# A fused linear-attention and mixer kernel: a subtraction on VectorE, tiles sorted by size, early reciprocals by way of DRAM, and products without a reader behind the early groups

## The chip, the cores and the metric

The kernel runs on one core of one Trainium2 chip. A core has a matrix engine (TensorE, in the profile PE, with PEld for its weight loads), and VectorE (DVE), ScalarE (ACT), GpSimd (POOL) and SyncE (SP), each with its own in-order queue of instructions. All data loads of the steady part are issued from SP. On chip, data lies in SBUF or in the eight banks of PSUM, into which the products are written. The metric is the device time of one execution in microseconds (us): the median of 3 runs of the kernel before is 1182.55 us.

## The reference, cut to what matters

```python
# q, k, v: (8, 8, 576, 64) float32; w_phi: (64, 128)
def phi(x):
    proj = np.einsum('bhsd,df->bhsf', x, w_phi)
    proj = proj - np.max(np.abs(proj), axis=-1, keepdims=True)
    return np.concatenate([np.exp(proj), np.exp(-proj)], axis=-1)
q_p, k_p = phi(q), phi(k)
kv = np.einsum('bhsf,bhsd->bhfd', k_p, v)
z = np.sum(k_p, axis=2)
num = np.einsum('bhsf,bhfd->bhsd', q_p, kv)
den = np.einsum('bhsf,bhf->bhs', q_p, z)[..., None] + 1e-06
x = (num / den)                      # then (B, S, H * D) = (8, 576, 512)
h = np.maximum(x.T @ w_tok1, 0.0) @ w_tok2        # token mixing, 576 -> 256 -> 576
u = x + h.T
out = u + np.maximum(u @ w_ch1, 0.0) @ w_ch2      # channel mixing, 512 -> 1536 -> 512
```

The subtraction in `phi` (the largest magnitude of a row off each of its 128 values) and the reciprocal of `den` are what the change touches.

## The kernel before, in words

There are 32 head pairs, numbered i = 0 to 31: four pairs (`NP`) for each of the eight batch entries. Five streams of work are written as Python generators and woven together by `weave` (L556): the keys of each pair (`keys`, L262: projection, subtraction, two exponentials `kp`, then products with v that sum up in `pkv`), its queries (`queries`, L325: projection, subtraction, transpose `pt`, exponentials `qf`, then the numerator products `pn` in `numerators`, L384), the token mixing of a batch entry, the loading of the mixer's weights (`load_weights`, L144), and the channel mixing. A planner then sets the order of the instructions on every engine when the program is built, from its own estimates of durations; on the chip each engine takes its queue in that order.

The weights come as float64. `convert` (L114) loads a block into one of four staging buffers, takes the magnitude on ACT (L131), rebuilds float32 bits on DVE in four instructions (L132 to L135), writes the rounded high part on ACT and the low part on POOL (`split`, L69 to L75). The 24 blocks of the channel weights are named `wc`.

The first four pairs (i < `PLAIN`) are computed with plain float32 products; `EARLY` = 8 covers the pairs of the first two batch entries. A group of keys or queries of an early plain pair goes through `less_max` (L191): one or two projections into half of a PSUM bank (L216), the row maximum on DVE (L226, `mx`), its negation on POOL (L229, `nmx`), and then, for keys, four ACT exponentials straight from PSUM that add `nmx` or `mx` as a bias, one for each unit and sign (L285); for queries an ACT pass for each unit that adds `nmx` (L235) and writes `pm`. From pair 4 on the values are subtracted on POOL (L237). Each plain pair has five groups of keys and five of queries: four with two units and one with one unit.

`numerators` takes one half of the sequence (k = 0: 320 columns, k = 1: 256) in two steps j. The rows of a `pn` bank hold 64 numerator rows and 64 copies of one denominator row; ACT copies the numerators into `x` (L404), the denominators plus 1e-6 go to `den` (L406 on ACT for the early pairs, L408 on DVE later). After j = 1 the reciprocal of the full 128-partition `den` is taken on DVE (L410) and POOL multiplies (L411). Token mixing begins with transposes of `x` (L432).

SBUF tiles come from two pools. Tiles that the matrix engine streams (`streamed`, L55) are padded by 16 elements on either side, and small columns to 32 elements (`column`, L65), so that every address keeps its offset within 128 bytes.

## Time and profile before

| | |
|---|---|
| median of 3 runs | 1182.55 us (1182.36 to 1184.48) |
| the profiled execution's own time | 1180.86 us |
| its span, first to last instruction | 1178.9 us |
| PE busy | 1134.0 us, 96% |
| DVE busy | 702.9 us, 60% |
| ACT busy | 673.5 us, 57% |
| POOL busy | 584.8 us, 50% |
| mean granted TensorE clock | 0.976 |

The spans leave out 2.0 us of the execution around the first and the last instruction. "Busy" counts an instruction from its start to its end, waits for a shared port included; a matrix product's end is modelled, so that products overlap. In the tables of groups, `out<-in` names the tiles, the count stands behind an x, then come total busy time, the mean in ns of one, and the idle time of the engine before them with what ended it. In the tables by stretch of time each engine's busy time has its count of instructions in brackets; then come the granted clock, the busy share of the DMA engines and their GB/s.

### The profile page before, as it was taken

The numbers are of one execution on the slowest core, as the hardware profiler recorded it, in microseconds if no ns is written. First come the engines' busy times: TensorE is split into PE (matmuls) and PEld (weight loads), VectorE is DVE, ScalarE is ACT, GpSimd is POOL, SyncE is SP. The second block draws the span as 40 slices with busy tenths as digits, with TensorE's granted clock in tenths as the row PEclk, the third lists the DMA queues.
The fourth block names the chain that finished last, engine by engine and source line by source line (L and its number), as shares of the span: only waits on it lengthen the run. The fifth ranks groups of instructions, "written<-read, shape, count | busy, mean of one in ns | idle before, by whom it ended". The sixth has DMA issues, their size and how long they took to land.

```text
span 1178.9 us, 24080 instructions
## 1 busy us (share of the span) xinstructions
PE 1134.0 (96%) x9032; PEld 1099.9 (93%) x9032; DVE 702.9 (60%) x1406; ACT 673.5 (57%) x1913; POOL 584.8 (50%) x774
## 2 busy tenths in 40 slices
PE   8877999999999999999999999999999999999998
PEld 6655889998999999998999999999999989999998
DVE  6899783566746666657656565474665666553111
ACT  6988784575746565566646455563665666441110
POOL 3567783465636564565546355462554655430000
PEclk9877799999999999999999999999999999999999
DMA  9543120111101111111111011110111110000000
GB/s 232 177 142 113 31 78 2 49 32 49 31 19 38 42 31 40 41 40 41 31 48 33 19 32 49 31 50 7 43 32 49 40 40 11 19 1 19 19 19 18
DMA packets 65299, 54.30 MB, mean 46 GB/s; under 512 B 44768, under 2 KB 56416, under 8 KB 65184
## 3 DMA queue, kind: packets, MB, share of 16 engines
q1 hardware_dynamic: 63824, 52.41, 15.4%
q8 instruction: 71, 1.16, 0.4%
q10 hardware_dynamic: 1360, 0.36, 0.1%
q14 instruction: 44, 0.36, 0.1%
HBM read 43.32 MB, written 9.44 MB: 45 GB/s over the span
## 4 chain that ended last, share of the span: by engine, by line
PE 84%; DVE 6%; ACT 6%; issue 2%; POOL 1%; DMA 1%; SPq 0%; POOLq 0%; DVEq 0%; ACTq 0%
PE acc L81 26%; PE h L81 26%; PE pkv L308 8%; PE pn L81 7%; PE ph L81 4%; PE pa L81 3%; PE pt L364 2%; PE ppk L212 2%; PE ppq L212 2%; DVE bitsc L135 1%; DVE bitsc L134 1%; PE px L432 1%; DVE bitsc L132 1%; ACT kp L285 1%; DVE den L410 1%
## 5 line engine op out<-in xcount | busy, mean ns | idle before, releaser
L81 PE MATMUL acc<-gh,wc 128*128 128x256 f32 x1728 | 339.7, 283 | 0.1
L81 PEld LDWEIGHTS acc<-gh,wc 128*128 128x128 f32 x1728 | 274.4, 188 | 0.4 <-ACT gh L498 0.4
L81 PE MATMUL h<-ul,wc_h 128*128 128x256 f32 x864 | 245.4, 284 | 1.9 <-POOL ul L479 1.8
L81 PE MATMUL h<-uh,wc_h 128*128 128x256 f32 x864 | 245.7, 285 | 0.5 <-DVE gl L499 0.5
L81 PE MATMUL h<-uh,wc_l 128*128 128x256 f32 x864 | 244.2, 283 | 0.0
L81 PE MATMUL acc<-gl,wc 128*128 128x256 f32 x864 | 243.2, 284 | 0.0
L308 PE MATMUL pkv<-v,kp 128*128 128x65 f32 (+1 forms) x1152 | 166.7, 280 | 6.9 <-ACT kp L285 4.3
L378 POOL TENSOR_TENSOR ql<-qf,qh 128x320 fp32r<-128x320 f32 (+1 forms) x112 | 93.0, 830 | 160.2 <-ACT qh L377 160.0
L308 PEld LDWEIGHTS pkv<-v,kp 128*128 128x128 f32 x1152 | 157.1, 202 | 14.6 <-ACT kp L285 7.9
L81 PEld LDWEIGHTS h<-ul,wc_h 128*128 128x128 f32 x864 | 162.8, 188 | 3.1 <-POOL ul L479 3.1
L81 PEld LDWEIGHTS h<-uh,wc_h 128*128 128x128 f32 x864 | 162.4, 188 | 1.1 <-DVE gl L499 1.1
L81 PEld LDWEIGHTS h<-uh,wc_l 128*128 128x128 f32 x864 | 163.2, 189 | 0.0
L81 PEld LDWEIGHTS acc<-gl,wc 128*128 128x128 f32 x864 | 162.9, 188 | 0.0
L499 DVE SCALAR_TENSOR_TENSOR gl<-h,gh 128x512 fp32r<-128x512 f32 x108 | 74.0, 685 | 144.1 <-ACT gh L498 143.1
L371 ACT ACTIVATE qf<-pt 128x320 f32<-128x320 f32 (+1 forms) x256 | 105.5, 416 | 85.9 <-PE pt L364 84.6
L282 ACT ACTIVATE kp<-pmk 128x256 f32<-128x256 f32 x280 | 96.0, 392 | 72.7 <-POOL pmk L237 69.6
L498 ACT ACTIVATE gh<-h 128x512 fp32r<-128x512 f32 x108 | 64.5, 598 | 112.8 <-PE h L81 112.1
L410 DVE RECIPROCAL den<-den 128x320 f32<-128x320 f32 x64 | 124.7, 1949 | 3.7 <-ACT den L406 2.3
L81 PE MATMUL pn<-qh,kv 128*128 128x320 f32 (+1 forms) x448 | 114.8, 297 | 0.6 <-ACT qh L377 0.3
L378 DVE TENSOR_TENSOR ql<-qf,qh 128x320 fp32r<-128x320 f32 (+1 forms) x112 | 70.1, 626 | 58.1 <-ACT qh L377 57.7
L237 POOL TENSOR_TENSOR pmk<-pk,mxk 128x256 f32<-128x256 f32 (+1 forms) x140 | 86.0, 614 | 35.7 <-DVE mxk L226 35.4
L187 POOL TENSOR_TENSOR stq<-raw,stq 64x512 fp32r<-64x512 f32 (+1 forms) x56 | 80.2, 1433 | 43.5 <-ACT stq L186 36.7
(112 smaller groups left out, 2418.4 us busy)
## 6 DMA issues: line engine op xcount, KB each, us to landing
raw<-in_qk SPq DMA_DIRECT2D x27, 576.0 KB, 3.8
rawc<-in_wc SPq DMA_DIRECT2D x24, 512.0 KB, 3.8
v<-in_vm SPq DMA_DIRECT2D x31, 256.0 KB, 3.4
out_x<-xt SPq DMA_DIRECT2D x12, 256.0 KB, 2.2
out_x<-xt SPq DMA_DIRECT2D x16, 192.0 KB, 2.0
raw<-in_w SPq DMA_DIRECT2D x8, 256.0 KB, 4.1
out_x<-xt SPq DMA_DIRECT2D x16, 128.0 KB, 1.9
pair<-in_qk SPq DMA_DIRECT2D x8, 160.0 KB, 4.5
```

Source lines behind the costliest of these rows:

```text
L81: nc.tensor.matmul(o, a, m, start=first and i == 0, stop=last and i == 2, skip_group_check=group_ok)
L187: nc.gpsimd.tensor_tensor(t[lo:lo + D], src, t[base:base + D].bitcast(F32), op=ALU.subtract)
L212: nc.tensor.matmul(ps[:, i].rearrange("p two f -> p (two f)"), t[:, c:c + P], wp2.rearrange("p two f -> p (two f)"), start=True, stop=True)
L237: nc.gpsimd.tensor_tensor(pm[:, :n], pr, mx[:, :n].unsqueeze(2).to_broadcast([P, n, F]), op=ALU.subtract)
L282: nc.scalar.activation(kp[:, :len(us), sg], pm[:, :len(us)], AF.Exp, scale=1.0 - 2.0 * sg)
L308: nc.tensor.matmul(o, kp[:, n, sg], v, start=g == 0 and n == 0 and sg == 0, stop=u is None, skip_group_check=True)
L364: nc.tensor.transpose(ptr[:, n], r, ident)
L371: nc.scalar.activation(full, src, AF.Exp, scale=1.0 - 2.0 * sg)
L378: (nc.gpsimd if sg else nc.vector).tensor_tensor(lo, full, hi.bitcast(F32), op=ALU.subtract)
L410: nc.vector.reciprocal(den, den)
L498: nc.scalar.activation(gh, ph, AF.Relu)
L499: nc.vector.scalar_tensor_tensor(gl, ph, 0.0, gh.bitcast(F32), op0=ALU.max, op1=ALU.subtract)
```

## The change: what it does

1. `less_max` for the plain pairs subtracts on DVE with one instruction for each group, from PSUM into the SBUF tile `pm`, for keys and queries alike. The negation on POOL, the bias forms of the exponential and the ACT pass of the queries are gone; the keys' exponentials take both units of a group in one instruction for each sign.
2. For i < `EARLY` the reciprocal goes by way of DRAM: the two distinct rows of `den` are written to a DRAM tile `row`, read back as a 128-partition tile `few` of 5 or 4 columns, inverted on DVE, written to `inv` in DRAM, and read back, each row 64 times, into `den`. That is six DMAs on SP and four transfers one behind the other, 16 times in all. `den` has two buffers in place of one.
3. Behind the last projection of each plain group, and behind the last product of each `pn` for i < `EARLY`, one more product of `wp2` with itself is written into a part of the same PSUM bank that nothing reads: 256 columns 40 times, 192 columns 32 times.
4. The padding of tiles is gone. Tiles are sorted into three SBUF pools: `cst`/`wk`, `st` for the streamed ones and `odd` for those whose size is no multiple of 512 bytes; two unused lead tiles of 32 and 192 bytes shift the first two.

```diff
+IDLE = 1
...
+    st = ctx.enter_context(tc.tile_pool(name="st", bufs=2))
+    odd = ctx.enter_context(tc.tile_pool(name="odd", bufs=2))
+    cst.tile([P, 8], F32, name="lead")
+    st.tile([P, 48], F32, tag="lead", name="lead2", bufs=1)
+    dr = ctx.enter_context(tc.tile_pool(name="dr", bufs=2, space=bass.MemoryType.DRAM))
...
-    w2_h = streamed(cst, [P, NT, S], F32R, name="w2_h")
+    w2_h = st.tile([P, NT, S], F32R, tag="w2_h", name="w2_h", bufs=1)
...
+    def idle(o, last):
+
+        n = o.shape[-1] * (o.shape[1] if len(o.shape) == 3 else 1)
+        with tc.issue_after(last.ins):
+            for _ in range(IDLE):
+                nc.tensor.matmul(o, wp2[:, 0], wp2.rearrange("p two f -> p (two f)")[:, :n],
+                                 start=True, stop=True, skip_group_check=True)
...
-                nc.tensor.matmul(ps[:, i, 0], t[rows, c:c + P], wp[rows], start=True, stop=True)
+                last = nc.tensor.matmul(ps[:, i, 0], t[rows, c:c + P], wp[rows], start=True, stop=True)
+        if base is not None:
+            idle(ps[:, :, 1], last)
...
-            pr = pr[:, :n]
+            pr, eng = pr[:, :n], nc.gpsimd
         else:
-            pr = ps[:, :n, 0]
-        mx = column(wk, 2, tag=f"mx{kind}", name=f"mx{name}")
+            pr, eng = ps[:, :n, 0], nc.vector
+        mx = odd.tile([P, 2], F32, tag=f"mx{kind}", name=f"mx{name}")
         nc.vector.tensor_reduce(mx[:, :n], pr, axis=AX.X, op=ALU.max, apply_absolute_value=True)
-        if base is not None:
-            nmx = column(wk, 2, tag="nmx", name=f"nmx{name}")
-            nc.gpsimd.tensor_scalar(nmx[:, :n], mx[:, :n], -1.0, None, op0=ALU.mult)
-        if base == D:
-            return pr, nmx, mx
         pm = wk.tile([P, 2, F], F32, tag=f"pm{kind}", name=f"pm{name}", bufs=1 if kind == "t" else 2)
-        if base == 0:
-            for i in range(n):
-                nc.scalar.activation(pm[:, i], pr[:, i], AF.Identity, bias=nmx[:, i:i + 1])
-        else:
-            nc.gpsimd.tensor_tensor(pm[:, :n], pr, mx[:, :n].unsqueeze(2).to_broadcast([P, n, F]), op=ALU.subtract)
+        eng.tensor_tensor(pm[:, :n], pr, mx[:, :n].unsqueeze(2).to_broadcast([P, n, F]), op=ALU.subtract)
         return pm
...
                 for sg in range(2):
-                    if i >= PLAIN:
-                        nc.scalar.activation(kp[:, :len(us), sg], pm[:, :len(us)], AF.Exp, scale=1.0 - 2.0 * sg)
-                        continue
-                    for n in range(len(us)):
-                        nc.scalar.activation(kp[:, n, sg], pm[0][:, n], AF.Exp, bias=pm[1 + sg][:, n:n + 1],
-                                             scale=1.0 - 2.0 * sg)
+                    nc.scalar.activation(kp[:, :len(us), sg], pm[:, :len(us)], AF.Exp, scale=1.0 - 2.0 * sg)
...
-            dens[0] = wk.tile([P, SEG[0][1]], F32, tag="den", name=f"den{i}_{k}", bufs=1)[:, :w]
+            dens[0] = odd.tile([P, SEG[0][1]], F32, tag="den", name=f"den{i}_{k}")[:, :w]
...
+        if i < EARLY:
+            idle(bank[:, SEG[0][1]:], last)
...
         if j == 1:
-            nc.vector.reciprocal(den, den)
+            if i < EARLY:
+
+                row, inv = (dr.tile([2, w], F32, tag=t, name=f"{t}{i}_{k}") for t in ("row", "inv"))
+                few = odd.tile([P, 8], F32, tag="few", name=f"few{i}_{k}")[:, :w // D]
+                for r in range(2):
+                    nc.sync.dma_start(row[r:r + 1], den[r * D:r * D + 1])
+                nc.sync.dma_start(few, row.rearrange("r (p c) -> (r p) c", c=w // D))
+                nc.vector.reciprocal(few, few)
+                nc.sync.dma_start(inv.rearrange("r (p c) -> (r p) c", c=w // D), few)
+                for r in range(2):
+                    nc.sync.dma_start(den[r * D:(r + 1) * D], inv[r:r + 1].to_broadcast([D, w]))
+            else:
+                nc.vector.reciprocal(den, den)
             nc.gpsimd.tensor_tensor(x, x, den, op=ALU.mult)
```

More of the change, by code (lines that the diff above doesn't have):

```diff
@@ L53, in mixer_kernel @@
     REST = dict(tag="rest", bufs=3)
-    def streamed(pool, shape, dtype, **kw):
-        n = 1
-        for k in shape[1:]:
-            n *= k
-        t = pool.tile([P, n + 32], dtype, **kw)[:, 16:16 + n]
-        if len(shape) == 3:
-            t = t.rearrange("p (a b) -> p a b", a=shape[1])
-        return t
-    def column(pool, n, **kw):
-        return pool.tile([P, 32], F32, **kw)[:, :n]
     def split(hi, lo, raw, eng_hi, eng_lo):
@@ L80, in mm3 @@
         for i, (a, m) in enumerate(((wh, xh), (wh, xl), (wl, xh))):
-            nc.tensor.matmul(o, a, m, start=first and i == 0, stop=last and i == 2,
-                             skip_group_check=group_ok)
+            r = nc.tensor.matmul(o, a, m, start=first and i == 0, stop=last and i == 2,
+                                 skip_group_check=group_ok)
+        return r
     ident = cst.tile([P, P], F32, name="ident")
     make_identity(nc, ident)
-    eps = cst.tile([P, 40], F32, name="eps")[:, :1]
+    eps = odd.tile([P, 1], F32, tag="eps", name="eps", bufs=1)
     nc.gpsimd.memset(eps, 1e-6)
-    wp2 = streamed(cst, [P, 2, F], F32R, name="wp2")
+    wp2 = st.tile([P, 2, F], F32R, tag="wp2", name="wp2", bufs=1)
     wp = cst.tile([P, F], F32, name="wp")
@@ L369, in turn @@
         for sg in range(2):
-            full = wk.tile([P, SEG[0][1]], F32, tag="qf", name=f"qf{i}_{k}{j}{sg}")[:, :w]
+            full = odd.tile([P, SEG[0][1]], F32, tag="qf", name=f"qf{i}_{k}{j}{sg}")[:, :w]
             nc.scalar.activation(full, src, AF.Exp, scale=1.0 - 2.0 * sg)
@@ L374, in turn @@
                 continue
-            hi = streamed(wk, [P, SEG[0][1]], F32R, tag="qh", name=f"qh{i}_{k}{j}{sg}")[:, :w]
-            lo = streamed(wk, [P, SEG[0][1]], F32R, tag="ql", name=f"ql{i}_{k}{j}{sg}")[:, :w]
+            hi = st.tile([P, 384], F32R, tag="qh", name=f"qh{i}_{k}{j}{sg}")[:, :w]
+            lo = st.tile([P, 384], F32R, tag="ql", name=f"ql{i}_{k}{j}{sg}")[:, :w]
             nc.scalar.activation(hi, src, AF.Exp, scale=1.0 - 2.0 * sg)
@@ L391, in numerators @@
         if j == 0:
-            dens[0] = wk.tile([P, SEG[0][1]], F32, tag="den", name=f"den{i}_{k}", bufs=1)[:, :w]
+            dens[0] = odd.tile([P, SEG[0][1]], F32, tag="den", name=f"den{i}_{k}")[:, :w]
         den = dens[0]
-        pn = ps_w.tile([P, SEG[0][1]], F32, **REST, name=f"pn{i}_{k}{j}")[:, :w]
+        bank = ps_w.tile([P, 512], F32, **REST, name=f"pn{i}_{k}{j}")
+        pn = bank[:, :w]
         for sg in range(2):
@@ L397, in numerators @@
             if i < PLAIN:
-                nc.tensor.matmul(pn, w_hl[0], qps[sg], start=sg == 0, stop=sg == 1)
+                last = nc.tensor.matmul(pn, w_hl[0], qps[sg], start=sg == 0, stop=sg == 1)
             else:
-                mm3(pn, w_hl, qps[sg], sg == 0, sg == 1)
+                last = mm3(pn, w_hl, qps[sg], sg == 0, sg == 1)
+        if i < EARLY:
+            idle(bank[:, SEG[0][1]:], last)
         rows, drows = slice(j * D, j * D + D), slice(D - j * D, P - j * D)
@@ L445, in token_mix @@
                 continue
-            xh = streamed(wk, [P, 2, P], F32R, tag="xh", name=f"xh{b}_{h}_{u}")[:w]
-            xl = streamed(wk, [P, 2, P], F32R, tag="xl", name=f"xl{b}_{h}_{u}")[:w]
+            xh = st.tile([P, 2, P], F32R, tag="xh", name=f"xh{b}_{h}_{u}")[:w]
+            xl = st.tile([P, 2, P], F32R, tag="xl", name=f"xl{b}_{h}_{u}")[:w]
             split(xh, xl, px[:w], nc.scalar, nc.vector)
@@ L473, in channel_mix @@
         for c in range(NC_):
-            h = streamed(wk, [P, CH], F32R, tag=f"uh{c}", name=f"uh{i}_{c}", bufs=1)
-            l = streamed(wk, [P, CH], F32R, tag=f"ul{c}", name=f"ul{i}_{c}", bufs=1)
+            h = st.tile([P, CH], F32R, tag=f"uh{c}", name=f"uh{i}_{c}", bufs=1)
+            l = st.tile([P, CH], F32R, tag=f"ul{c}", name=f"ul{i}_{c}", bufs=1)
             d = 0
```

12 lines of the change are left out of this document (6 added, 6 removed).

## The prediction

> **What bounds the kernel now.** I read the table by stretches of time first, with cuts where the load of the engines changes.
>
> ```profile
> 0.00:30.00 30.00, 24.80 (x103) 20.23 (x103) 19.40 (x46) 18.70 (x54) 12.29 (x33) 1.00 0.93 235
> 30.00:128.00 98.00, 79.68 (x368) 61.84 (x367) 92.50 (x138) 82.01 (x222) 62.25 (x69) 0.75 0.42 128
> 128.00:177.00 49.00, 45.39 (x329) 42.19 (x330) 37.13 (x81) 41.10 (x117) 40.06 (x48) 0.95 0.23 65
> 177.00:1178.90 1001.90, 984.14 (x8237) 975.60 (x8235) 553.90 (x1144) 531.64 (x1523) 470.16 (x627) 1.00 0.11 31
> ```
>
> From 177 us on PE is busy 984.14 of 1001.90 us at full clock: every product added there costs its time, and relief of other engines is worth little. Before it PE stands for 5 to 18 us in each stretch, and at 30 to 128 us its clock is 0.75. There DVE is busy 92.50 of 98.00 us. The chain of waits, cut to 20 to 128 us, names the same engine:
>
> ```profile
> by line: DVE bitsc L134 11.7%; DVE bitsc L135 11.1%; DVE bitsc L132 9.0%; issue 8.4%; DVE den L410 7.4%; ACT kp L285 6.2%; DVE bitsc L133 6.0%; PE pn L398 6.0%; DMA rawc<-in_wc 5.2%; PE pkv L308 4.4%; ACT bitsc L131 2.8%; PE ppq L216 2.4%;
> ```
>
> The rebuilding of the mixer weights (`bitsc`, L132 to L135), the full reciprocals (`den` L410) and the keys' exponentials (`kp` L285) lead. So the end is set by how early DVE is through with this stretch; what it gains there moves everything behind it, since PE then runs full. Last I read the groups of the stretch, the order of time, and the queue of SP.
>
> **The change part by part.** *The subtraction.* These are DVE's groups from 30 to 128 us, then rows in order of time, which give what an instruction takes from the queue, start to start:
>
> ```profile
> L135 DVE SCALAR_TENSOR_TENSOR bitsc<-rawc,bitsc 128x512 uint32<-128x512 uint32 x23 | 21.0, 916 | 0.2
> L134 DVE SCALAR_TENSOR_TENSOR bitsc<-rawc,bitsc 128x512 uint32<-128x512 uint32 x22 | 19.8, 899 | 0.2
> L132 DVE TENSOR_SCALAR bitsc<-bitsc 128x512 f32<-128x512 f32 x22 | 15.5, 704 | 1.1 <-ACT bitsc L131 1.1
> L133 DVE TENSOR_SCALAR bitsc<-bitsc 128x512 uint32<-128x512 uint32 x22 | 14.5, 659 | 0.2
> L410 DVE RECIPROCAL den<-den 128x320 f32<-128x320 f32 x4 | 8.6, 2144 | 0.0
> L410 DVE RECIPROCAL den<-den 128x256 f32<-128x256 f32 x4 | 7.0, 1741 | 0.0
> L221 DVE TENSOR_TENSOR pk<-ppk,partk 128x256 f32<-128x256 f32 x4 | 1.7, 414 | 0.0
> ```
>
> ```profile
> 39.14 2.15 DVE L410 RECIPROCAL den<-den 128x320 f32<-128x320 f32 x1
> 41.20 0.36 DVE L132 TENSOR_SCALAR bitsc<-bitsc 128x512 f32<-128x512 f32 x1
> ...
> 119.40 0.68 DVE L135 SCALAR_TENSOR_TENSOR bitsc<-rawc,bitsc 128x512 uint32<-128x512 uint32 x1
> ...
> 120.33 0.41 DVE L133 TENSOR_SCALAR bitsc<-bitsc 128x512 uint32<-128x512 uint32 x1
> 120.67 0.41 DVE L75 TENSOR_TENSOR xl<-px,xh 128x256 fp32r<-128x256 f32 x1
> 121.00 0.41 DVE L221 TENSOR_TENSOR pk<-ppk,partk 128x256 f32<-128x256 f32 x1
> 121.33 1.04 DVE L133 TENSOR_SCALAR bitsc<-bitsc 128x512 uint32<-128x512 uint32 x1
> ...
> 128.32 0.28 DVE L221 TENSOR_TENSOR pk<-ppk,partk 128x128 f32<-128x128 f32 x1
> ```
>
> Plain pairs have 4 x 8 groups of two units and 4 x 2 of one, so 40 new subtractions. The nearest row has the same shape and a PSUM input (L221): 0.33 us start to start (121.00 to 121.33), 0.41 in duration; with one unit I take 0.20, its 0.28 less the same 0.08 of overlap. That is 32 x 0.33 + 8 x 0.20 = 12.2 us (by durations 15.4).
>
> *The reciprocals.* All eight of the plain pairs lie in this stretch, 8.6 + 7.0 = 15.6 us, or 15.0 with 0.08 of overlap each (39.14 to 41.20 is 2.06, not 2.15). From the two shapes, (2144 - 1741) / 64 = 6.3 ns a column and 0.13 us besides; five columns cost an estimated 0.16 us, start to start 0.08, so 8 x 0.08 = 0.6 us. DVE's sum: 12.2 + 0.6 - 15.0 = -2.2 us (by durations 15.4 + 1.3 - 15.6 = +1.1). I take -2: in a full queue starts count. The other eight reciprocals fall at 128 to 265 us, where DVE has room (37.13 of 49.00); I take -0.4, between 0 and the 49.00 - 45.39 = 3.6 us that PE stands there.
>
> *The negations.* POOL loses 40, ACT the bias passes:
>
> ```profile
> L229 POOL TENSOR_SCALAR nmxq<-mxq 128x2 f32<-128x2 f32 x13 | 5.3, 404 | 9.6 <-DVE mxq L226 6.4 <-ACT kp L285 3.2
> L229 POOL TENSOR_SCALAR nmxk<-mxk 128x2 f32<-128x2 f32 x10 | 3.6, 359 | 2.6 <-DVE mxk L226 2.5
> L285 ACT ACTIVATE kp<-ppk,mxk 128x128 f32<-128x128 f32 x24 | 7.9, 384 | 0.0
> L285 ACT ACTIVATE kp<-ppk,nmxk 128x128 f32<-128x128 f32 x23 | 7.4, 370 | 0.1
> L282 ACT ACTIVATE kp<-pmk 128x256 f32<-128x256 f32 x8 | 2.9, 406 | 0.0
> L235 ACT ACTIVATE pmq<-ppq,nmxq 128x128 f32<-128x128 f32 x28 | 9.1, 384 | 0.5 <-POOL nmxq L229 0.4
> ```
>
> ```profile
> 31.17 0.21 POOL L229 TENSOR_SCALAR nmxk<-mxk 128x2 f32<-128x2 f32 x1 [1.13 <-DVE mxk L226]
> ```
>
> ACT's work falls by 72 x 0.377 - 32 x 0.406 - 8 x 0.377 + 36 x 0.384 = 25 us; it was busy 82.01 of 98.00 and off DVE's path, but a group's way from maximum to product loses the POOL hop and half the exponentials. DVE stands 98.00 - 92.50 = 5.5 us in this stretch, most of it for products that wait on such chains: worth 0 to -5.5, I take -2. On the negations themselves: L132 and L133 take 0.41 us unopposed (120.33) but 0.70 and 0.66 in the mean, L134 and L135 0.90 and 0.92 against 0.68 (119.40): 1.0 us for each of 22 to 23 blocks, 22 us lost to something. The two groups of negations shown are 8.9 of POOL's 62.25 busy us, 14%; 14% of 22 is 3. Bounds: 0, if they are not the cause, and 40 x 0.21 = -8.4. I take -3.
>
> The Trainium skill (SBUF — State Buffer, "Who interferes with whom") says that only a shared port pair causes such loss: a DVE instruction in a two-port mode or with two SBUF inputs and a GpSimd one block each other whole, and a DVE instruction with at most one SBUF input outside those modes is free. By it the new subtraction (PSUM and one SBUF input) is never held up, and the -3 stands; but the reciprocals were free too, and POOL worked unopposed beside them, so taking 15 us of them away against 12 us of free subtractions returns about 3/98 of the 22 us, +0.7. The trace fits the rule (0.41 and 1.04 for the same L133); no run here has isolated it.
>
> *The products without a reader.* 56 of 72 fall in the plain groups, where PE stands 98.00 - 79.68 = 18 us: cost 0. The last 16 (192 columns) fall on pairs 4 to 7, mostly after 140 us. The nearest price is the pace of 256-column products:
>
> ```profile
> 171.00 0.28 PE L81 MATMUL h<-ul,wc_h 128*128 128x256 f32 x1
> ...
> 171.94 0.28 PE L81 MATMUL h<-uh,wc_h 128*128 128x256 f32 x1
> ```
>
> Eight starts in 0.94 us, 0.1175 each; 192 columns by proportion 0.088; 16 x 0.088 = +1.4 us. Bounds: 0 if all fall into gaps, 72 x 0.1175 = +8.5 with no cover. If a reader of the bank must wait for the product (40 x 0.12 = 4.7 us), DVE's conversions fill that time. In the same eight products the rows of `uh` and `ul` pass, padded tiles of 1152 bytes whose addresses differ modulo 512 if laid side by side; the pace is even. The sorted tiles keep the offsets modulo 128 (lead tiles of 32 and 32 + 192 bytes), so I take 0 for *the sorting*. The rounding of those starts leaves 0.01 / 8 us open either way, times 8237 products after 177 us: +-10 us as bounds.
>
> *The way by DRAM.* Six DMAs a time; four transfers one behind the other. The nearest are the 16 KB `vt` loads, at 20 to 128 us and after 300 us, and this is what SP does in the stretch:
>
> ```profile
> v<-in_vt SPq DMA_DIRECT2D x8, 16.0 KB, 3.0
> ...
> v<-in_vt SPq DMA_DIRECT2D x40, 16.0 KB, 2.0
> ```
>
> ```profile
> SPq L125 <- DVE bitsc L135: 54.4, 16, 8.6
> ...
> 69.11 1.13 SPq L274 DMA_DIRECT2D v<-in_vt  x2
> ```
>
> From `den` to `few`: one issue of 0.56 us (1.13 for two) ahead of the second row, then two landings of 3.0: 6.6 us; then `inv` and two reads back, 0.56 + 2 x 3.0 more, 13.1 us in all against 2. The transposes that read `x` have room:
>
> ```profile
> 127.59 1.06 POOL L411 TENSOR_TENSOR xt<-xt,den 128x256 f32<-128x256 f32 x1
> ...
> 147.71 0.38 PE L432 MATMUL px<-ident,xt 128*128 128x128 f32 x2
> ```
>
> The last multiplication of batch 0 ends at 128.65; the transposes of that half begin at 147.71, 19 us later, more than the 11 us added. Without that cover the whole 11 us would stand once for each batch entry. What can hurt is the queues. The small reciprocal sits in DVE's order; if `few` has not landed, DVE stands, and behind it the conversions, maxima and subtractions, for which ACT's exponentials, POOL's low halves and PE wait. On SP each of three dependent transfers holds up the loads of `wc` behind it; but SP already waits 54.4 us for DVE to free staging buffers, 3.4 us at a time, so loads have that slack, and they in turn can hold up `few`. On POOL the multiplication waits for the last landing, with low halves behind it, and POOL has 36 us of room in 98. How far off the planner put the reciprocal I can't see: 0 if it allowed 6.6 us, 6.6 - 2 x 2.0 = 2.6 us each, 8 x 2.6 = +21, if it allowed only the quiet landing of 2.0. I take +2, nearer to the lower end, because DVE's longest stand in that stretch is for PE:
>
> ```profile
> DVE mxq L226 <- PE ppq L216: 2.1, 2, 1.8
> ```
>
> The 5.2% of the chain that are landings of `rawc` show that the upper end isn't excluded.
>
> *Sum:* -2 - 0.4 - 2 - 3 + 1.4 + 2 = -4.0 us on the profiled execution: 1180.86 to 1176.9 (span 1174.9 and 2.0 around it). That execution lies 1.7 us under the median of 1182.55, so the median should come to 1178.5. With the bounds of the taken terms its own range is 1172 to 1182.
>
> **The rivals.** *DVE stands for `few`* (slower). Place: the eight early halves in the DVE-bound stretch. At 2.0 us each it costs 16 in place of 2: -4.0 - 2 + 16 = +10, 1192.5; it decides from 6.0 / 8 = 0.75 us each. For it: landings of 3.0 us in this stretch, SP waits of 3.4 us ahead of them, and a DVE that is full, so that no stand is made up. Against it: conversions slowed by POOL give the transfers more time than a planner that counts them unopposed.
>
> *The gain is hidden* (no change). POOL's multiplication stands for the last landing, holding low halves and through them DVE's buffers, or the planner's new order wastes as much elsewhere: the 4 us of DVE's sum come back, 1182.5. For it: each term is a few us in a stretch of 98. Against: POOL's 36 us of room.
>
> *The clock holds* (much faster). The products without a reader lift the clock.
>
> ```profile
> 90.00:95.00 5.00, 5.00 (x18) 4.06 (x17) 4.10 (x8) 4.18 (x13) 3.68 (x5) 0.50 0.40 111
> ...
> 140.00:145.00 5.00, 4.66 (x36) 4.22 (x36) 2.54 (x7) 4.73 (x13) 4.01 (x6) 1.00 0.00 0
> ```
>
> ```profile
> 8.44 1.97 PE L308 MATMUL pkv<-v,kp 128*128 128x65 f32 x8
> ...
> 140.22 1.00 PE L308 MATMUL pkv<-v,kp 128*128 128x65 f32 x8
> ```
>
> The first columns of products take 1.97 us cold and 1.00 warm. If PE were warm from 8 us on, I put 5 us on the first 30 (DVE busy 19.40 of 30), the 3.5 us left of DVE's stands, and 0.05 x 49 = 2.5 us at 128 to 177: -4.0 - 11 = -15, 1167.5. Against it: at 90 to 95 us the clock is 0.50 with PE busy all the time but 18 products; at 1.00 it starts 36. One more for each group of eight to ten hardly changes that.
>
> By the Trainium skill (TensorE: Matmul & The Clock Gate, "HAM oscillation — how this bites in real kernels") the clock falls only after an idle gap of more than some 3.4 us. The row at 90 to 95 us, 0.50 with PE busy 5.00 of 5.00, does not agree; by the rule the products would matter only where they break such a gap.
>
> **How the numbers follow.** My forecast, 1178.5, gets 0.40; DVE standing 0.32; hidden 0.14; the clock 0.10; the rest (a new order far off either way) 0.04. 0.2% is 2.4 us, about what tells a change from none here: faster means under 1180.2, slower over 1184.9. The forecast gives 0.34 faster and 0.06 same, the clock 0.10 faster, hidden 0.11 same and 0.03 slower, standing 0.29 slower and 0.03 same, the rest half and half: 0.46, 0.20, 0.34. The range goes from the clock's 1168 to stands of 2.5 us, 1196.
>
> **What would show it.** Right: no DVE idle ended by a DMA at the small reciprocal; L132 to L135 with means nearer 0.41 and 0.68; the conversions over some 7 us before 128; PE busy after it at the same pace. Wrong: waits of DVE on `few`, or of POOL on `den`, of over 6 us in all; PE products of 256 columns at another pace than 0.1175 after 177 us, which would be the sorting; a clock over 0.9 at 30 to 128 us.

## The result and the profile after

The changed kernel takes 1173.55 us (median of 20 runs, 1167.99 to 1194.77) against 1182.32 us for the kernel before beside it (20 runs, 1179.02 to 1184.48). The ratio is 0.9934, with a 95% interval of 0.9914 to 0.9953: some 8 us faster (8.8 by the medians), and a spread several times as wide as before. The ratios and intervals here leave out executions over 1.5% above the fastest of their kernel, the medians don't; the profiles of e3 and e9 are of such executions. The profiled execution took 1180.92 us with a span of 1178.8, so it lies 7 us above the median and shows no gain over the 1180.86 us of the execution profiled before. What it shows is therefore where time moved.

The table by stretches of time, changed kernel, same cuts as in the prediction (columns: stretch, its length, busy time with count of PE, PEld, DVE, ACT and POOL, granted clock, busy share of the DMA engines, GB/s):

```profile
0.00:30.00 30.00, 25.00 (x86) 19.78 (x86) 18.40 (x49) 13.01 (x30) 9.04 (x21) 1.00 0.74 186
30.00:128.00 98.00, 91.75 (x418) 74.09 (x417) 79.92 (x157) 67.59 (x166) 43.02 (x34) 0.78 0.49 142
128.00:177.00 49.00, 42.41 (x270) 39.14 (x270) 37.38 (x81) 35.63 (x98) 35.16 (x38) 0.84 0.27 79
177.00:1178.90 1001.90, 983.53 (x8335) 974.91 (x8334) 552.81 (x1161) 543.61 (x1553) 483.01 (x642) 1.00 0.12 33
```

At 30 to 128 us PE and DVE have changed places: PE is busy 91.75 us (79.68 before), DVE 79.92 (92.50 before). The line of the chain of waits from 20 to 128 us says the same:

```profile
by line: PE pkv L299 18.3%; PE pn L390 15.0%; PE ppk L219 12.1%; PE ppq L219 10.3%; PE ppk L191 5.4%; PE ppq L191 4.8%; DMA few<-row 4.6%; issue 4.5%; DVE bitsc L129 4.5%; PE pt L355 4.2%; DVE bitsc L130 3.9%; DVE bitsc L127 2.0%; PE ppt L2
```

The conversions and reciprocals on DVE that led it before have shrunk, products lead (`pkv`, `pn`, the projections), and 10.2% are products without a reader (`ppk`, `ppq` of L191; that line is the helper that issues them). The groups of the same stretch:

```profile
L130 DVE SCALAR_TENSOR_TENSOR bitsc<-rawc,bitsc 128x512 uint32<-128x512 uint32 x19 | 17.4, 914 | 0.0
L129 DVE SCALAR_TENSOR_TENSOR bitsc<-rawc,bitsc 128x512 uint32<-128x512 uint32 x19 | 16.3, 859 | 0.0
...
L128 DVE TENSOR_SCALAR bitsc<-bitsc 128x512 uint32<-128x512 uint32 x19 | 13.4, 706 | 0.1
...
L127 DVE TENSOR_SCALAR bitsc<-bitsc 128x512 f32<-128x512 f32 x20 | 13.2, 660 | 2.5 <-ACT bitsc L126 2.5
...
L191 PE MATMUL pn<-wp 128*128 128x192 f32 x15 | 9.3, 617 | 0.0
...
L191 PE MATMUL ppk<-wp 128*128 128x256 f32 x14 | 6.7, 479 | 0.0
L191 PE MATMUL ppq<-wp 128*128 128x256 f32 x13 | 6.2, 473 | 0.0
...
L233 DVE TENSOR_TENSOR pmq<-ppq,mxq 128x256 f32<-128x256 f32 x13 | 5.4, 413 | 1.3 <-PE pt L355 1.3
L231 DVE TENSOR_REDUCE mxq<-ppq 128x2 f32<-128x256 f32 x13 | 5.3, 412 | 5.3 <-PE ppq L191 5.3
...
L233 DVE TENSOR_TENSOR pmk<-ppk,mxk 128x256 f32<-128x256 f32 x11 | 4.6, 414 | 0.0
L231 DVE TENSOR_REDUCE mxk<-ppk 128x2 f32<-128x256 f32 x11 | 4.5, 417 | 3.1 <-PE ppk L191 3.1
...
L411 DVE RECIPROCAL few<-few 128x5 f32<-128x5 f32 x4 | 0.7, 175 | 0.0
...
L411 DVE RECIPROCAL few<-few 128x4 f32<-128x4 f32 x3 | 0.5, 173 | 1.3 <-DMA few<-row 1.3
```

DVE converts 19 to 20 blocks in this stretch instead of 22 to 23, so the conversions end later, not earlier: the last instruction of the last block ends at 175 us, at 165 us before. The rows of a product without a reader last 473 to 617 ns, and the row maxima (L231) wait for such products, 5.3 and 3.1 us in all.

That rows of 177 us to the end look alike (983.53 us busy then, 984.14 before) hides a second difference. It appears when the last 100 us are cut off and products are counted. First the kernel before:

```profile
0.00:177.00 177.00, 149.87 (x798) 124.26 (x799) 149.03 (x262) 141.81 (x391) 114.60 (x148) 0.85 0.46 129
177.00:1077.00 900.00, 886.20 (x7407) 877.86 (x7406) 537.17 (x1118) 518.26 (x1497) 464.46 (x619) 1.00 0.12 33
1077.00:1300.00 223.00, 97.94 (x833) 97.74 (x831) 16.73 (x26) 13.38 (x26) 5.70 (x8) 0.99 0.02 8
```

Then the changed kernel:

```profile
0.00:177.00 177.00, 159.15 (x771) 133.01 (x772) 135.70 (x286) 116.23 (x292) 87.23 (x93) 0.84 0.47 132
177.00:1077.00 900.00, 885.68 (x7474) 877.26 (x7474) 534.75 (x1132) 529.89 (x1526) 476.64 (x632) 1.00 0.12 35
1077.00:1300.00 223.00, 97.85 (x864) 97.65 (x862) 18.06 (x29) 13.72 (x28) 6.37 (x10) 0.99 0.02 8
```

By 177 us the changed kernel has issued 771 products, of which 60 have no reader: 711 useful ones against 798. In the 900 us behind that it issues 7474 against 7407 in the same busy time, and in its last stretch 864 in 97.85 us where the kernel before issues 833 in 97.94. Divided out, a product costs 885.68 / 7474 = 118.5 ns in the middle (before 119.6) and 113.2 ns at the end (before 117.6). So in this execution the changed kernel loses some 87 x 0.118 = 10 us early and wins about as much back by a faster pace of PE. The experiments show which part of the change does which.

### The profile page after: what moved, and what is told of

Its sections match the earlier page's. It is cut to its first block, busy times and chain, and to the rows that moved or that the text cites. A ratio compares the mean times of both kernels' runs of the same rounds, so it can differ in the third digit from the quotient of the medians.

```text
span 1178.8 us, 24278 instructions
## 1 busy us (share of the span) xinstructions
PE 1142.7 (97%) x9104; PEld 1107.9 (94%) x9104; DVE 688.5 (58%) x1446; ACT 659.8 (56%) x1845; POOL 570.2 (48%) x734
## 4 chain that ended last, share of the span: by engine, by line
PE 89%; ACT 5%; DVE 3%; issue 1%; DMA 1%; POOL 1%; SPq 0%; DVEq 0%; POOLq 0%; ACTq 0%
PE acc L75 26%; PE h L75 25%; PE pkv L299 10%; PE pn L75 7%; PE ph L75 3%; PE pa L75 3%; PE pt L355 3%; PE ppk L215 2%; PE ppq L215 2%; PE pn L390 1%; PE ppk L219 1%; PE px L438 1%; PE ppq L219 1%; ACT qh L368 1%; DVE bitsc L129 1%
## 5 line engine op out<-in xcount | busy, mean ns | idle before, releaser
L75 PE MATMUL acc<-gh,wc 128*128 128x256 f32 x1728 | 334.1, 281 | 0.2 <-ACT gh L504 0.2
L75 PE MATMUL h<-ul,wc_h 128*128 128x256 f32 x864 | 242.9, 281 | 2.5 <-POOL ul L485 2.3
L299 PE MATMUL pkv<-v,kp 128*128 128x65 f32 (+1 forms) x1152 | 164.3, 279 | 0.0
L277 ACT ACTIVATE kp<-pmk 128x256 f32<-128x256 f32 (+1 forms) x320 | 109.4, 392 | 87.1 <-POOL pmk L233 75.1
L417 POOL TENSOR_TENSOR xt<-xt,den 128x320 f32<-128x320 f32 x64 | 53.3, 832 | 105.8 <-DVE den L416 39.2
```

Source lines behind the costliest of these rows:

```text
L75: r = nc.tensor.matmul(o, a, m, start=first and i == 0, stop=last and i == 2, skip_group_check=group_ok)
L277: nc.scalar.activation(kp[:, :len(us), sg], pm[:, :len(us)], AF.Exp, scale=1.0 - 2.0 * sg)
L299: nc.tensor.matmul(o, kp[:, n, sg], v, start=g == 0 and n == 0 and sg == 0, stop=u is None, skip_group_check=True)
L417: nc.gpsimd.tensor_tensor(x, x, den, op=ALU.mult)
```

## The experiments

The ratios are to runs of the kernel before on the same chip in the same batch (medians 1181.55, 1180.19 and 1180.48 us). "Useful by 177" are the products issued in the first 177 us less those without a reader; the last two columns are PE's busy time divided by its products, in ns, from 177 to 1077 us and from there to the end. Each is read from one profile a kernel; those of e3 and e9 are left out of the table, and e3's last stretch is read by itself further below.

| kernel | median us | ratio (95%) | useful by 177 | ns, middle | ns, end |
|---|---|---|---|---|---|
| before | 1182.32 | | 798 | 119.6 | 117.6 |
| changed | 1173.55 | 0.9934 (0.9914-0.9953) | 711 | 118.5 | 113.2 |
| e1 changed, again | 1172.29 | 0.9909 (0.9878-0.9940) | 720 | 118.4 | 113.3 |
| e2 no product without reader | 1165.40 | 0.9865 (0.9832-0.9898) | 868 | 118.6 | 113.2 |
| e3 full reciprocals | 1176.86 | 0.9964 (0.9942-0.9985) | | | |
| e4 old subtraction | 1178.70 | 0.9973 (0.9958-0.9988) | 721 | 118.5 | 113.3 |
| e5 sorted tiles alone | 1167.18 | 0.9890 (0.9874-0.9907) | 805 | 118.3 | 113.2 |
| e6 sorted, new subtraction | 1167.89 | 0.9897 (0.9884-0.9910) | 807 | 118.4 | 113.3 |
| e7 sorted, reciprocals by DRAM | 1178.96 | 0.9986 (0.9969-1.0002) | 746 | 118.5 | 113.2 |
| e8 products of 32 columns | 1167.19 | 0.9870 (0.9849-0.9892) | 833 | 118.5 | 113.2 |
| e9 sorted, one `den` buffer | 1171.39 | 0.9918 (0.9895-0.9942) | | | |
| e10 sorted, streamed tiles 128 bytes longer | 1179.54 | 0.9998 (0.9985-1.0011) | 800 | 119.7 | 117.3 |
| e11 sorted, streamed tiles shifted by 256 bytes | 1170.56 | 0.9921 (0.9907-0.9934) | 829 | 118.5 | 117.7 |
| e12 sorted, streamed tiles at the weights' offset | 1192.31 | 1.0110 (1.0089-1.0131) | 754 | 121.0 | 120.9 |

### One part taken out of the changed kernel

**e1**, the changed kernel unchanged.

> The changed kernel once more, unaltered, for a second profile: the one at hand is of an execution of 1180.9 us, 7 us over the median of 1173.6. If the spread of the changed kernel comes from the clock of TensorE (cold stretches that start at another place in each execution), a profile near 1170 us shows a granted clock over 0.85 at 30 to 128 us (0.78 in the one at hand) and PE no longer busy all the time at 70 to 100 us. If it comes from late landings on the way by DRAM, the clock is the same and the waits of DVE for few and of POOL for den are shorter than 8.6 and 19.4 us.

It gives 0.9909 (0.9878 to 0.9940), which overlaps the interval of the first measurement (0.9914 to 0.9953). The second profile is again of an execution above the median (1179.21 us); it shows nearly the same clock at 30 to 128 us (0.79) and no shorter waits for the way by DRAM, so what makes the spread stays open.

**e2**, without the products that nothing reads.

```diff
-IDLE = 1
+IDLE = 0
```

> The changed kernel without the products that nobody reads. My sum has them cost 1.4 us: about 1172. If they are what keeps the clock up, without them the gain goes: 1180 to 1183 and a clock near 0.976 for the whole span. If, in cold stretches, they cost PE the 0.5 us each that the profile at hand shows, this is faster: 1165 to 1170, and more even.

1165.40 us: against e1 the products cost 7 us by the medians and 5 by the ratios, whose intervals overlap a little. The stretch from 30 to 128 us of e2:

```profile
30.00:128.00 98.00, 77.52 (x412) 62.19 (x412) 90.90 (x176) 74.17 (x181) 53.00 (x43) 0.83 0.54 154
```

PE is busy 77.52 us with 412 products, all of them useful, where the changed kernel is busy 91.75 us with 418, of which 45 have no reader (the 42 shown above and 3 of `ppt`). The clock is 0.83 here and 0.78 with them (0.79 in e1): in these profiles they do not raise it.

**e3**, the changed kernel with the reciprocal of the full tile on DVE.

```diff
-            if i < EARLY:
-                row, inv = (dr.tile([2, w], F32, tag=t, name=f"{t}{i}_{k}") for t in ("row", "inv"))
...
-            else:
-                nc.vector.reciprocal(den, den)
+            nc.vector.reciprocal(den, den)
```

> The changed kernel with the reciprocals of the early groups on the full tile on DVE again. By DVE's sum it has 15 us more in the stretch to 128 us: if DVE sets its end, 1180 to 1188. If PE or the clock sets it, less than 4 us over the changed kernel. If late landings hold the changed kernel up, this is faster and its spread smaller.

1176.86 us, 0.9964. Against e1 in the same batch (0.9909) the way by DRAM is worth 4.6 us here, where new subtraction and products stand beside it; the two intervals only just part.

**e4**, the changed kernel with the negation on POOL and the bias forms on ACT.

```diff
-        eng.tensor_tensor(pm[:, :n], pr, mx[:, :n].unsqueeze(2).to_broadcast([P, n, F]), op=ALU.subtract)
+        if base is not None:
+            nc.gpsimd.tensor_scalar(nmx[:, :n], mx[:, :n], -1.0, None, op0=ALU.mult)
...
+                nc.scalar.activation(pm[:, i], pr[:, i], AF.Identity, bias=nmx[:, i:i + 1])
```

> The changed kernel with the negation on POOL and the bias passes on ACT again, all else kept. DVE has 12 us less work in the stretch: if DVE's sum sets the end, faster than the changed kernel by 5 to 10 us, 1164 to 1168. If the shorter chain and the free port are worth more (my terms of 2 and 3 us) it is within 2 us of it. If ACT or POOL is next in line, slower: 1176 to 1182.

1178.70 us, 0.9973: with the way by DRAM and the products in place, the new subtraction is worth 6.4 us. Against e7, which has the old subtraction and the way by DRAM but no products without a reader (0.9986), e4 shows no cost of these products; beside the new subtraction and full reciprocals (e3 against e6, 0.9964 to 0.9897) they cost about 8 us.

### One part put into the kernel before

**e5**, the kernel before with the three pools and the lead tiles (and `den` in two buffers), nothing else.

```diff
+    st = ctx.enter_context(tc.tile_pool(name="st", bufs=2))
+    odd = ctx.enter_context(tc.tile_pool(name="odd", bufs=2))
+    cst.tile([P, 8], F32, name="lead")
+    st.tile([P, 48], F32, tag="lead", name="lead2", bufs=1)
...
-            gh = streamed(wk, [P, 2, CH], F32R, tag="g", name=f"gh{i}_{ep}", bufs=4)
+            gh = st.tile([P, 2, CH], F32R, tag="g", name=f"gh{i}_{ep}", bufs=4)
```

> The kernel before with the tiles sorted and den in two buffers, and none of the other parts. My term for the sorting is 0: 1182 within 2 us, and the pace of the 256-column products after 177 us stays 0.1175 us. If the place of tiles matters to PE, the pace and the time differ by up to 10 us.

1167.18 us, 13.0 us under its kernel before: more than the whole change gains. The profile shows where:

```profile
0.00:177.00 177.00, 154.63 (x805) 128.47 (x806) 145.93 (x258) 140.14 (x383) 111.64 (x143) 0.84 0.44 124
177.00:1077.00 900.00, 886.20 (x7489) 877.91 (x7488) 542.09 (x1126) 523.35 (x1508) 469.40 (x624) 1.00 0.12 34
1077.00:1300.00 223.00, 84.24 (x744) 84.04 (x742) 14.66 (x23) 11.55 (x23) 5.73 (x8) 0.99 0.02 7
```

The early part is that of the kernel before (805 products by 177 us, 798 before). The middle and the end run at the pace of the changed kernel, 118.3 and 113.2 ns. For the 8233 products behind 177 us that is 7489 x 1.31 + 744 x 4.4 ns = 13.1 us, the measured gain.

**e6**, e5 with the new subtraction.

```diff
+            pr, eng = ps[:, :n, 0], nc.vector
...
-            nmx = odd.tile([P, 2], F32, tag="nmx", name=f"nmx{name}")
-            nc.gpsimd.tensor_scalar(nmx[:, :n], mx[:, :n], -1.0, None, op0=ALU.mult)
...
+        eng.tensor_tensor(pm[:, :n], pr, mx[:, :n].unsqueeze(2).to_broadcast([P, n, F]), op=ALU.subtract)
```

> Sorted tiles and the subtraction on DVE; reciprocals on the full tile, no products without a reader. By DVE's sum it has 12 us more in the stretch to 128 us, less 3 for the port and 2 for the chain: 1189. If DVE's queue isn't what sets the end but the way from projection to product, faster than before: 1174 to 1178, by the 6 us that this part gained inside the changed kernel.

1167.89 us against 1167.18: nothing gained or lost. It answers one step by itself: does DVE convert faster when POOL no longer negates? The conversion groups on DVE, 30 to 128 us, first of e5, where POOL negates for each plain group:

```profile
L130 DVE SCALAR_TENSOR_TENSOR bitsc<-rawc,bitsc 128x512 uint32<-128x512 uint32 x21 | 22.7, 1081 | 0.2
...
L129 DVE SCALAR_TENSOR_TENSOR bitsc<-rawc,bitsc 128x512 uint32<-128x512 uint32 x20 | 17.0, 848 | 0.3
...
L127 DVE TENSOR_SCALAR bitsc<-bitsc 128x512 f32<-128x512 f32 x21 | 13.4, 640 | 0.5 <-ACT bitsc L126 0.4
...
L128 DVE TENSOR_SCALAR bitsc<-bitsc 128x512 uint32<-128x512 uint32 x21 | 12.9, 613 | 0.1
```

Then of e6, where it never does:

```profile
L129 DVE SCALAR_TENSOR_TENSOR bitsc<-rawc,bitsc 128x512 uint32<-128x512 uint32 x20 | 19.8, 990 | 0.0
...
L127 DVE TENSOR_SCALAR bitsc<-bitsc 128x512 f32<-128x512 f32 x19 | 15.2, 798 | 0.8 <-ACT bitsc L126 0.8
L130 DVE SCALAR_TENSOR_TENSOR bitsc<-rawc,bitsc 128x512 uint32<-128x512 uint32 x19 | 14.4, 756 | 0.0
...
L128 DVE TENSOR_SCALAR bitsc<-bitsc 128x512 uint32<-128x512 uint32 x20 | 12.8, 638 | 0.0
```

The four means add up to 3182 ns a block in e5 and to 3182 in e6. Single rows move, which may go with the order in which POOL's work falls beside them, but the sum doesn't; over all 24 blocks of the whole execution it is 3130 ns in e5 and 3149 in e6. In these two executions the negations are not what slows the conversions.

**e7**, e5 with the way by DRAM.

```diff
-            nc.vector.reciprocal(den, den)
+            if i < EARLY:
+                row, inv = (dr.tile([2, w], F32, tag=t, name=f"{t}{i}_{k}") for t in ("row", "inv"))
...
+                    nc.sync.dma_start(den[r * D:(r + 1) * D], inv[r:r + 1].to_broadcast([D, w]))
```

> Sorted tiles and the reciprocals by way of DRAM; negations on POOL and bias passes on ACT, no products without a reader. By DVE's sum 15 us less on DVE: 1168 to 1172 if it sets the end, and better than the version with the subtraction too (1165) if that costs DVE 12 us. By the chain theory the part alone gains at most 4 us: 1178.

1178.96 us, 11.8 us slower than e5, though DVE has lost its 15 us of reciprocals. Its row of the stretch, and its chain of waits from 20 to 128 us:

```profile
30.00:128.00 98.00, 75.72 (x349) 58.58 (x349) 73.62 (x136) 80.20 (x216) 58.10 (x67) 0.76 0.47 137
```

```profile
by line: DMA den<-inv 9.1%; PE pkv L313 8.9%; PE pn L404 8.6%; DMA inv<-few 7.8%; issue 5.7%; DMA row<-den 5.4%; DVE bitsc L129 5.3%; PE ppk L219 4.2%; DMA few<-row 3.8%; ACT kp L290 3.8%; DVE bitsc L128 3.8%; DVE bitsc L130 3.0%; ACT den L
```

DVE is busy 73.62 of 98.00 us and PE 75.72: no engine is full, all wait. The four transfers (`row`, `few`, `inv`, `den`) make 5.4 + 3.8 + 7.8 + 9.1 = 26.1% of the chain. By 177 us e7 has issued 59 useful products less than e5, 7 us at 0.119 each, part of the 11.8. POOL's multiplication waits for `den`, and in e7 POOL's queue also holds the negations that the next groups need; in e2, with the subtraction on DVE, the groups do not pass POOL. That this is why the way by DRAM costs 11.8 us beside the old subtraction and nothing beside the new one (e2, 1165.40 us, against e6, 1167.89 us) fits both kernels, but no run moved that queue by itself. It is not the length of POOL's own waits, which are no shorter in e2. First e2, then e7, first 177 us:

```profile
POOL xt L417 <- DMA den<-inv: 15.2, 9, 3.5
```

```profile
POOL xt L431 <- DMA den<-inv: 13.2, 6, 4.9
```

### The length of the products

**e8**, the changed kernel with products of 32 columns in place of 256 and 192.

```diff
-            idle(ps[:, :, 1], last)
+            idle(ps[:, 0, 1, :32], last)
...
-            idle(bank[:, SEG[0][1]:], last)
+            idle(bank[:, SEG[0][1]:SEG[0][1] + 32], last)
```

> The changed kernel with each product without a reader cut to 32 columns (256 and 192 before). If their cost of 7 us is PE's time for the columns, most of it goes: 1166 to 1168. If it is the wait of the reader for one more instruction and its weight load, it stays: 1171 to 1173.

1167.19 us. The same 72 products at a sixth to an eighth of the columns give back some 5 of the 7 us by the medians, so it looks to be mostly their length that costs, not that they are there; the intervals of e8 and e1 still touch. Its row of 30 to 128 us:

```profile
30.00:128.00 98.00, 85.56 (x474) 70.71 (x474) 88.21 (x177) 74.70 (x187) 50.99 (x44) 0.90 0.56 162
```

The clock is 0.90 here, 0.83 with no such product and 0.78 with the long ones, and PE's busy time is 85.56, 77.52 and 91.75 us: in these three profiles the clock followed neither the number of products nor PE's busy time. The time was no better than that of e2.

### What it is in the sorting

The built programs give every tile an address. Offsets within 512 bytes, of the tiles that PE streams in the channel mix (`uh`, `ul`, `gh`, `gl`) and of the weights `wc`, and with them the distance modulo 512:

| kernel | streamed | weights | distance |
|---|---|---|---|
| before | 96, 224, 352, 480 | 160, 288, 416 | all of 64, 192, 320, 448 |
| changed, e1 to e9 | 352 | 160 | 192 |
| e10 | 96, 224, 352, 480 | 160 | 448, 64, 192, 320 |
| e11 | 96 | 160 | 448 |
| e12 | 160 | 160 | 0 |

All but e12 keep the distance of 64 within 128 bytes that the kernel before was built around. From the changed kernel on the weights lie at 160 throughout: no run moves them alone.

**e9**, e5 with one buffer of `den`.

```diff
-            dens[0] = odd.tile([P, SEG[0][1]], F32, tag="den", name=f"den{i}_{k}")[:, :w]
+            dens[0] = odd.tile([P, SEG[0][1]], F32, tag="den", name=f"den{i}_{k}", bufs=1)[:, :w]
```

> The kernel before with the sorted tiles alone, but with one den buffer again as before. Theory (the place of the tiles is the whole gain): 1167 us, within 2 us of the sorted kernel's 1167.2, and 90 products per 10 us at 1080 to 1160 us. Rival (the second den buffer is the gain): back to about 1180, since the order in the early part is that of before.

0.9918 (0.9895 to 0.9942), against 0.9890 (0.9874 to 0.9907) with two buffers: the intervals overlap, so the second buffer is worth between nothing and a few us. By the ratios three quarters of e5's gain stand without it. In the built programs e9's products stand in the order of the kernel before, all 8352 of them, so this much of the gain is not a matter of order. The 1171.39 us lie outside the 2 us that were expected.

**e10**, e5 with each streamed tile 128 bytes longer, used from its start.

```diff
+    def padded(shape, dtype, **kw):
...
+        t = st.tile([P, n + 32], dtype, **kw)[:, :n]
...
-            gh = st.tile([P, 2, CH], F32R, tag="g", name=f"gh{i}_{ep}", bufs=4)
+            gh = padded([P, 2, CH], F32R, tag="g", name=f"gh{i}_{ep}", bufs=4)
```

> The kernel before with the sorted tiles, but each streamed tile 128 bytes longer: the offset within 128 bytes stays 96, while the offsets within 512 bytes are 96, 224, 352 and 480 again as in the kernel before, in place of 352 alone; the weights stay at 160 alone. Theory 1 (one offset within 512 bytes for all streamed tiles makes the pace): about 1180, 87 products per 10 us at 1080 to 1160. Theory 2 (the weights' common offset, or that sizes are sorted at all, makes it): 1167 and 90 products. Theory 3 (each pair of streamed and weight offset has its own pace): in between, 1170 to 1178, with different paces for products of different tiles.

1179.54 us, 0.9998: the whole gain is gone, with pools, weights, lead tiles, `den` and the order of all products as in e5. The pace is that of before:

```profile
177.00:1077.00 900.00, 886.51 (x7406) 878.17 (x7405) 540.17 (x1125) 522.70 (x1507) 469.48 (x624) 1.00 0.12 34
1077.00:1300.00 223.00, 97.47 (x831) 97.27 (x829) 16.74 (x26) 13.40 (x26) 5.73 (x8) 0.99 0.02 8
```

**e11** and **e12**, e5 with a longer second lead tile: 448 bytes (all streamed tiles 256 bytes further) and 512 bytes (streamed tiles at the offset of the weights).

```diff
-    st.tile([P, 48], F32, tag="lead", name="lead2", bufs=1)
+    st.tile([P, 112], F32, tag="lead", name="lead2", bufs=1)
```

```diff
-    st.tile([P, 48], F32, tag="lead", name="lead2", bufs=1)
+    st.tile([P, 128], F32, tag="lead", name="lead2", bufs=1)
```

> The kernel before with the sorted tiles, the second lead tile 256 bytes longer: streamed tiles at 96 within 512 bytes in place of 352, weights at 160 as before. If only the regularity counts: 1167 within 2 us. If the distance of the streamed tile to the weights within 512 bytes sets the pace: another time, over 1172 or under 1163, and another pace at 1080 to 1160 us than 90 products per 10 us.

> The kernel before with the sorted tiles, the second lead tile 512 bytes long: streamed tiles at 160 within 512 bytes, the very offset of the weights, and at 32 within 128 in place of 96. If the distance of 64 within 128 bytes, which the kernels before and after keep, counts: slower than 1180. If no distance counts and only regularity does: 1167 within 2 us.

e11 takes 1170.56 us, which fits neither of its two expectations. Its pace is that of e5 in the middle (886.16 / 7480 = 118.5 ns) and that of before at the end (85.56 / 727 = 117.7):

```profile
177.00:1077.00 900.00, 886.16 (x7480) 877.89 (x7480) 540.20 (x1124) 521.67 (x1503) 466.75 (x621) 1.00 0.12 34
1077.00:1300.00 223.00, 85.56 (x727) 85.35 (x725) 14.65 (x23) 11.60 (x23) 5.70 (x8) 0.99 0.02 8
```

e12 takes 1192.31 us, slower than the kernel before, with 121.0 ns in the middle and 120.9 at the end (its profile is of an execution 7 us above the median):

```profile
177.00:1077.00 900.00, 887.51 (x7335) 879.79 (x7335) 534.87 (x1114) 525.79 (x1514) 471.74 (x625) 1.00 0.12 33
1077.00:1300.00 223.00, 114.51 (x947) 113.76 (x945) 24.46 (x41) 16.00 (x33) 7.06 (x11) 0.99 0.03 10
```

So neither the pools nor the even sizes make the gain: e10 has both, and only the offset at which PE's streamed operands lie differs from e5. It might be read as a pace for each distance from the weights, with 192 bytes best. The traces say otherwise. These are 50 us of the last stretch, in which only products of the channel mix run, of e5 (distance 192), e11 (448), e3 (192, the same addresses as e5) and the kernel before, in this order (a product that crosses an edge is counted):

```profile
1110.00:1160.00 50.00, 50.00 (x444) 50.00 (x443) 7.61 (x11) 6.68 (x13) 2.87 (x4) 1.00 0.04 12
1110.00:1160.00 50.00, 50.00 (x427) 50.00 (x426) 7.61 (x11) 6.70 (x13) 2.85 (x4) 1.00 0.04 12
1110.00:1160.00 50.00, 50.00 (x427) 50.00 (x426) 8.45 (x15) 7.81 (x17) 5.70 (x8) 1.00 0.07 22
1110.00:1160.00 50.00, 50.00 (x427) 50.00 (x427) 8.30 (x12) 7.29 (x14) 2.85 (x4) 1.00 0.04 14
```

e5 starts 444 products, the others 427. With e5's very addresses e3 runs at e11's pace here, at least in its profiled execution of 1193.56 us. How that can be shows when the starts of the 5184 products of the channel mix, which the traces hold to the nanosecond, are put beside the addresses of the built programs. Between 177 and 1077 us an unbroken run of such products goes at one of two paces in e5 and in e11 alike, about 113.3 or about 117.8 ns from start to start. By the mean of each run of nine or more, 54% of the products lie at 113.2 to 114.0 in e5 and 48% in e11, the others at 117.6 to 117.9, and none between. In e11 the 31 products from 327.14 us on take 113.4 ns each and the 32 from 455.85 us on 117.7; at the same places of the program e5 has the same two. The last stretch is one long such run: at 113.3 in e5, at 117.8 in e11 and e3. In e12 nearly all lie at 119.0 to 120.0. In e10 and the kernel before, where the offset changes from product to product, 97% and 93% lie at 117 to 118.5 and none under 116, and the distance of a product from its weights makes little of it: in the last stretch of e10 the 177 products at a distance of 192 take 116.9 ns, those at 64, 320 and 448 take 117.9, 117.7 and 116.8.

What the mixture loses, then, is the faster of the two paces that one fixed offset allows. Whether 192 is better than 448 is not shown: the ratios of e5 and e11 meet at 0.9907, e9 in e11's own batch has 0.9918 at 192, and the slower pace in the last stretch of e11's profile is worth 727 x 4.5 ns = 3.3 us, about what lies between their medians (3.4). What decides between the two paces stays open. So does what is special in e12, which changes the offset within 128 bytes too (32 in place of 96), and whether the distance from the weights counts at all or only the streamed operand's own offset, since no run moved the weights alone. The longer lead tiles shift the `odd` pool too, by 256 and 320 bytes, but the products of the channel mix read only `st` tiles and weights.

By the Trainium skill (SBUF — State Buffer, "Who interferes with whom") PE has two read ports, one for the streamed operand and one for the weight load, independent of each other. Moving the streamed tiles alone changes the pace from 113.3 to 120.0 ns here; whether the two reads meet, these runs don't show. The Trainium skill (TensorE: Matmul & The Clock Gate, "Wait — 56ns, not 53.3ns?") puts warm products of N columns back to back at N / 2.4 GHz and some 2.5 ns apart, an estimated 109.2 ns for 256 columns. Here each product has a weight load of its own, and the faster pace comes within some 4 ns of that, while the others stay 8 to 11 ns above it.

## Why the prediction was right in its time and wrong in its reasons

1178.5 us was forecast, 1173.55 came, within the range and on the side that was called likelier. But the sum's -4.0 us was not made of what makes up the measured -8.8: one term of it that stood at 0 was -13, and nearly all that was counted as gain came to little.

**The sorting, 0.** This step failed. It read eight starts in 0.94 us at 171 us, 0.1175 each, called the pace even over rows whose addresses differ modulo 512, and concluded that offsets modulo 512 don't count. An even pace over a mixture only shows that the mixture is even; it says nothing of what one fixed distance would give. The end of the kernel before, 97.94 / 833 = 117.6 ns, is the same pace; with one fixed offset it is 113.2 in e5. The measured term is -13.0 (e5), outside even the +-10 that the rounding left open. e10 shows that what was lost is the mixture modulo 512, the very thing the step dismissed. The place to look was named right, "another pace than 0.1175 after 177 us, which would be the sorting".

**The products without a reader, +1.4.** This term was mis-sized: 5 to 8 us (the ratio of e2 against those of e1 and of the first measurement). They were priced at 0.1175 us, the pace of products at full clock, and 56 of them were taken as covered by the 18 us in which PE stood. But in that stretch the clock is 0.78, and from the start of such a product to PE's next start it is 0.32 us at the median for 256 columns and 0.52 for 192. The prediction's own rows of cold and warm products, 1.97 and 1.00 us, would make some 0.23 of 0.1175; what makes up the rest was not taken apart. Both covers failed at once: PE filled up, and DVE stood for them (5.3 and 3.1 us in the rows of L231) where the step let conversions fill the time. That they cost nothing beside the old subtraction (e4 against e7) the step could not say.

**Subtraction, reciprocals and the shorter chain, -2 and -2.** The prices of the single instructions held: `pm` on DVE 413 and 414 ns in two-unit form (0.41 forecast), the small reciprocals 175 and 173. DVE's sum moved as forecast too: between 30 and 128 us e7 takes 16.2 us from e5's 89.82, and e6 fills DVE to 93.52 while it converts a block or two less. But a lower sum of the fullest engine was turned into time one for one, and that step did not hold: e7 frees 16 us of DVE and gets slower; only both parts together gain, e2 against e5 0.9865 to 0.9890, with overlapping intervals, so -3 us or nothing.

**The negations, -3.** Not there: 3182 ns a block with and without (e5, e6). The share of POOL's busy time was taken as a share of the loss. The rule of the Trainium skill on the shared port (SBUF — State Buffer, "Who interferes with whom"), which the step quoted, speaks of instructions that meet, not of busy shares; that a new order moves the rows by 25 to 325 ns and leaves their sum as it was does not contradict it, and no run here isolates the meeting itself.

**The way by DRAM, +2.** The waits of the changed kernel for it, first 177 us:

```profile
POOL xt L417 <- DMA den<-inv: 7.5, 6, 2.2
...
DVE few L411 <- DMA few<-row: 1.7, 3, 1.1
```

DVE stands 1.7 us for `few`, near the 2 of the forecast (4.5 us in e1, the same kernel), and the cover ahead of the transposes held: none of the products that transpose `x` waits. POOL's 7.5 us are above the 6 that the prediction named as a sign of being wrong, and cost nothing that the runs can show, as POOL is busy 43.02 of 98.00 us. With the new subtraction the way by DRAM is no loss (-4.6 by e1 against e3, -2.5 by e2 against e6); without it it costs +11.8, which the prediction could not see, since it costed each edit alone against the kernel before and not in the presence of the others.

**The rivals.** DVE standing for `few` did not happen in the changed kernel. It did in e4, where the old subtraction stands beside the way by DRAM, first 177 us:

```profile
DVE few L425 <- DMA few<-row: 11.0, 4, 5.4
```

In e7 DVE's stands for `few` come to 4.0 us, but all four transfers are on the chain. The clock did not hold:

```profile
90.00:95.00 5.00, 5.00 (x20) 4.26 (x20) 3.21 (x9) 2.85 (x7) 2.08 (x2) 0.50 0.09 34
```

0.50 with PE busy 5.00 of 5.00 us, as before. The rule of the Trainium skill (TensorE: Matmul & The Clock Gate, "HAM oscillation — how this bites in real kernels") that the prediction weighed there, by which an idle gap of more than some 3.4 us lowers the clock, does not agree here either. In the changed kernel the clock falls to 0.50 at 68.7 us, and from 10 us up to there PE has not once stood for over 1 us:

```profile
65.00:68.60 3.60, 3.60 (x22) 2.79 (x22) 3.42 (x7) 3.27 (x9) 1.60 (x2) 1.00 0.76 257
68.80:72.00 3.20, 3.20 (x13) 2.84 (x13) 3.18 (x7) 3.17 (x9) 1.83 (x2) 0.50 0.60 208
```

The gain was hidden in one sense: subtraction, reciprocals and products together turn e5's 1167 into 1173.

**What would have been read off the changed profile.** The conversions over 7 us earlier, and faster: neither. No DVE idle at the small reciprocal: nearly. The same pace behind: no, and that was the sign that told.

## What to carry to other kernels

Where one engine runs full for most of the time, count its instructions in equal stretches of two profiles and divide: a pace that differs by 1% was worth more here than any wait, and a busy row of 100% doesn't show it. Where only the sum over a stretch is counted, two paces can hide in one mean, so look at the starts of single instructions too. Give the streamed operands one offset modulo 512 bytes, and try several; padding that keeps only an offset within 128 bytes leaves 13 us here. And price a filler instruction by rows of the stretch in which it runs: without the 72 products (e2, 1165.40 us) this kernel beats both versions, and the sorted tiles alone (e5, 1167.18) do all but 2 us of that.
